# A fixed order with the last token group's output pairs at the end, norm arithmetic on ScalarE, and ten warm-up matmuls instead of fifteen

## The chip, the cores and the metric

The kernel runs on one core of one Trainium2 chip. The metric is device time in microseconds of one execution. Engines are named as in the profile: PE (TensorE, with PEld for its weight loads), DVE (VectorE), ACT (ScalarE), POOL (GpSimd) and SP (SyncE, which only issues DMAs here).

## The reference

Two branches read the same x = `A_q` of 2048 tokens by 640 columns (B_x is not read). One is a long convolution along the tokens, done in the kernel by matrix products with folded Fourier matrices; the other is a token-shifting MLP with two norms. A gate per token mixes them.

```python
kv = (4-tap shift convolution of k with shift_k) * v
y = irfft(rfft(kv padded to 2S) * rfft(ssm_k padded)) [:S] + kv * ssm_D
a = q * y

h = gelu(layernorm(x) @ w1)          # 640 x 640
hs = concat(four column quarters of h, shifted by +1, -1, +2, -2 tokens) @ w2
x1 = x + hs
b = x1 + gelu(layernorm(x1) @ w3) @ w4   # 640 x 1536, 1536 x 640

g = sigmoid((x * gate_w).sum(-1))
return g * a + (1 - g) * b           # x is A_q in both branches
```

## The kernel before

The kernel does not issue instructions directly. Its functions record operations (`P.op`, `P.dma`) with what they read and write; each gets a number in the order of recording. `SEQUENCE`, a list of these numbers written into the source, is the order in which the operations are put on their engines. Each engine works strictly in that order, and waits on semaphores for what its next operation needs. In the kernel before, `schedule` walks the list with estimated durations to choose a PSUM bank for each result, and to hold some large loads behind an earlier transfer; the estimates change nothing else.

Tokens are worked in 16 tiles of 128 (t), in groups of four (sc or c). The columns of the convolution come in two halves of 320 (g or hh). The steps that the change and the prediction touch are these.

- Constants and warm-up: fifteen 512-column matmuls on a buffer of ones (line 715), a first Gelu that loads ScalarE's table (718), and `taps` (four-tap weights spread over partitions by PE).
- `ln1`, `bn_math`: the first norm. DVE's statistics (857, 858), then variance plus epsilon on DVE or POOL (674), then the power -0.5 on POOL (861). `mm1` multiplies by w1. ACT applies Gelu; the fifth block of 128 rows goes to a buffer `hx`, from which DVE copies four 32-row pieces to their shifted places (924).
- `mm2`, `ln2`: w2, x1 and its sums. In `ln_math` POOL makes the mean and a product, DVE the difference, POOL the power; for tiles 8 and up POOL also makes an offset. Then the normed rows go to SP's transposing DMA.
- `mm3`, `mm4`: w3 with Gelu, w4. `base` scales x1 by (1 - g) and stores it, and `mm4`'s result is added to it in memory by an accumulating DMA from POOL's queue. Where a half of a tile is not "summed" there, PE adds x1 with an identity matmul, and the row is kept on the chip.
- `kv_half`, `kv_block`, `x_fwd`, `combine`: the taps and products on DVE, a flip by PE, the forward transform. `h_load`, `h_fold`, `h_chunk`: the same for the filter.
- `unit(hh, c)`: the block products in the frequency domain, all large DVE operations.
- `final(hh, c, q, k)`: the inverse transform of a pair of token tiles by PE, ACT's copy, DVE's sum and difference, a flip by PE, ACT's scaled copy, and DVE's product with q. For k under 12 the pair is added in memory by POOL's accumulating DMA; the last four add X on DVE and are stored by SP.

All DVE tensor-tensor operations have line 669, all matmuls of `mm` line 689, all ACT activations of `act` line 679, all tensor-scalar operations of `ts` line 674, all DMA issues line 237. The transposes of `ln1` on PE have line 903, and the addition of x in `mm2` line 959.

Of the kernel before, what the change touches and what calls it, by code (L numbers as in the profile page):

```python
# [12 lines left out]
class Op:  # L13
    __slots__ = ("idx", "eng", "fns", "ins", "outs", "dur", "bias", "nbytes", "preds", "succs", "rank",
                 "tp", "early", "cost", "free", "grp", "tile", "ordinal", "waits", "inc", "value", "dsem", "dval", "snap", "snapd", "start", "end", "order", "lat")

    def __init__(self, idx, eng, fns, ins, outs, dur, bias, nbytes):
        self.idx = idx
        self.eng = eng
        self.fns = fns  # L20
        self.ins = ins
        self.outs = outs
        self.dur = dur
        self.bias = bias
        self.nbytes = nbytes
        self.preds = {}
        self.succs = []
        self.inc = False
        self.dsem = None
        self.tp = False  # L30
        self.early = False
        self.cost = 0.0
        self.lat = 0.0
        self.free = None
        self.tile = None
# [87 lines left out]
def regions(ap):  # L123
# [30 lines left out]
    for lo, hi in runs:  # L154
        b0, b1 = (f0 + lo) * esz, (f0 + hi) * esz
        for q in range(p0 // 32, (p0 + pcnt - 1) // 32 + 1):
            out.add(("SB", q, b0, b1))
# [16 lines left out]
class Prog:  # L174
# [51 lines left out]
    def dma(self, queue, out, in_, bias=0.0, transpose=False, slow=False, free=None, early=False, accum=False, fn=None):  # L226
# [11 lines left out]
        issue = (350.0 + n / 90.0) if transpose else (970.0 if queue == "pool" else 470.0)  # L238
# [5 lines left out]
        op.cost = n * esz / 256 * 1.65 if transpose else n * esz / run * ((46 + 0.087 * run) if accum else (8 + 0.0435 * run)) / 16  # L244
        op.lat = 1150.0 if transpose else 3000.0 if accum else 2300.0
# [8 lines left out]
    def edges(self):  # L254
        out = []
        for o in self.ops:
            row = []
            for p in o.preds:
                q = self.ops[p]
                if q.nbytes:  # L260
                    d = 60.0
                elif q.eng == o.eng:
                    d = 0.0 if o.eng == "pe" else 120.0
                else:
                    d = {"pe": 205.0, "dve": 120.0, "act": 130.0, "pool": 60.0, "sp": 60.0}[q.eng]
                    d += {"pe": 65.0, "pool": 60.0}.get(o.eng, 0.0)
                row.append((p, d))
            out.append(row)
        return out

    def schedule(self, sequence, backlog=3000.0):
        ops = self.ops
        delays = self.edges()
        free = {"pe": 1580.0, "act": 720.0, "dve": 930.0, "pool": 1190.0, "sp": 720.0}
        dfree = 0.0
        done = []
        avail = [0.0] * 8
        tenant = [None] * 8
        todo = {t.idx: len(t.users) for t in self.banks}
        last = {t.idx: 0.0 for t in self.banks}  # L280
        order = []
        for i in sequence:
            o = ops[i]
            st = max([free[o.eng]] + [ops[p].end + d for p, d in delays[i]])
            if o.nbytes and not o.tp and not o.early:
                st = max(st, dfree - backlog)
            t = o.tile
            if t is not None and t.place is None:
                free_at = {b: max(avail[b:b + t.n]) for b in range(0, 8, t.n)}
                st = max(st, min(free_at.values()))  # L290
                assert st < 1e17, "no bank"
                t.place = min((avail[b ^ 1] <= st if t.n == 1 else False, a, b) for b, a in free_at.items() if a <= st)[2]
                for b in range(t.place, t.place + t.n):
                    if tenant[b] is not None:
                        for u in tenant[b].users:
                            if ops[u].eng != "pe":
                                o.preds.setdefault(u, False)
                    tenant[b] = t
                    avail[b] = 1e18
            o.start = st  # L300
            free[o.eng] = st + o.dur
            o.end = st + o.dur
            if o.nbytes:
                dfree = max(st + 0.5 * o.dur, dfree) + o.cost
                o.end = max(dfree, o.end) + o.lat
                if o.cost > 500 and not o.tp and not o.early:
                    gate = [(ops[d].end, d) for d in done if ops[d].end <= st]
                    if gate:
                        o.preds.setdefault(max(gate, key=lambda g: g[0])[1], False)
                done.append(i)  # L310
            if t is not None:
                todo[t.idx] -= 1
                last[t.idx] = max(last[t.idx], o.end)
                if todo[t.idx] == 0:
                    for b in range(t.place, t.place + t.n):
                        avail[b] = last[t.idx] + 195.0
# [147 lines left out]
def bass_gated_mix__ssm_conv_h3__mixer_s_mlp__prompt_kernel(  # L464
# [33 lines left out]
    def ps(n, cls):  # L498
# [3 lines left out]
    SEQUENCE = [2, 3, 10, 11, 12, 31, 6, 57, 8, 1, 13, 14, 15, 16, 17, 18, 19, 20, 21, 22, 23, 24, 25, 7, 9, 0, 4, 28, 5, 56, 29, 63, 58, 64,  # L502
                59, 27, 141, 30, 60, 35, 61, 52, 65, 62, 76, 66, 26, 80, 67, 34, 77, 42, 68, 78, 70, 146, 53, 82, 69, 71, 43,
                44, 46, 83, 79, 48, 50, 73, 81, 142, 321, 72, 47, 144, 301, 74, 75, 96, 205, 98, 86, 97, 84, 39, 87, 36, 143,
                147, 85, 89, 99, 92, 106, 145, 37, 88, 54, 41, 108, 204, 599, 93, 148, 158, 45, 40, 149, 157, 55, 90, 116,
                161, 120, 249, 160, 250, 102, 109, 113, 162, 136, 91, 137, 150, 154, 138, 139, 151, 159, 103, 302, 117, 38,
                140, 94, 112, 114, 107, 322, 303, 219, 304, 122, 305, 121, 130, 163, 118, 164, 165, 600, 49, 115, 155, 131,
                152, 126, 123, 168, 124, 156, 127, 221, 104, 119, 128, 218, 207, 153, 100, 125, 132, 101, 166, 167, 179, 134,
                169, 171, 222, 110, 51, 223, 133, 308, 210, 170, 135, 111, 209, 177, 129, 95, 601, 323, 199, 220, 224, 200,
                33, 206, 266, 306, 172, 324, 606, 185, 307, 208, 607, 602, 175, 176, 193, 187, 201, 105, 328, 202, 180, 181,  # L510
                211, 212, 405, 603, 267, 178, 188, 213, 194, 182, 203, 425, 173, 264, 186, 268, 196, 191, 192, 183, 604, 406,
                407, 174, 184, 251, 426, 415, 198, 631, 318, 416, 608, 319, 214, 263, 427, 609, 408, 252, 409, 610, 225, 435,
                428, 325, 195, 417, 630, 611, 315, 418, 326, 316, 265, 436, 632, 215, 637, 309, 429, 430, 431, 432, 216, 341,
                317, 437, 320, 633, 197, 455, 310, 438, 456, 228, 419, 638, 605, 226, 327, 311, 634, 612, 217, 445, 420, 189,
                457, 254, 269, 446, 458, 229, 253, 270, 635, 312, 255, 639, 613, 313, 338, 227, 190, 342, 339, 447, 661, 314,
                459, 460, 461, 343, 448, 365, 465, 340, 329, 330, 615, 614, 344, 410, 640, 236, 421, 466, 238, 345, 641, 32,
                616, 642, 237, 331, 256, 346, 663, 367, 617, 664, 257, 662, 366, 239, 636, 234, 668, 242, 235, 232, 258, 665,
                233, 411, 348, 467, 230, 385, 347, 369, 243, 332, 333, 666, 241, 261, 240, 643, 259, 670, 244, 245, 468, 246,
                247, 370, 644, 335, 336, 412, 475, 692, 248, 231, 334, 671, 645, 337, 296, 271, 476, 672, 469, 485, 260, 477,
                478, 507, 669, 508, 368, 387, 509, 273, 693, 479, 262, 699, 371, 449, 357, 486, 627, 628, 629, 487, 358, 359,  # L520
                673, 386, 496, 497, 624, 498, 480, 646, 372, 701, 422, 360, 481, 361, 389, 625, 626, 667, 489, 413, 362, 674,
                675, 353, 354, 356, 450, 451, 694, 618, 619, 355, 390, 423, 349, 620, 350, 363, 364, 373, 272, 274, 374, 700,
                279, 452, 351, 695, 676, 621, 462, 439, 440, 622, 375, 352, 658, 659, 648, 280, 696, 470, 388, 697, 275, 283,
                677, 655, 660, 647, 623, 441, 442, 702, 289, 290, 291, 292, 704, 652, 276, 424, 653, 656, 414, 443, 284, 705,
                649, 650, 703, 678, 706, 651, 287, 657, 732, 392, 293, 285, 433, 277, 698, 654, 391, 278, 471, 707, 294, 281,
                733, 402, 282, 295, 286, 472, 708, 709, 689, 297, 288, 298, 690, 679, 403, 518, 396, 397, 519, 404, 300, 482,
                734, 710, 434, 711, 680, 739, 735, 691, 713, 511, 512, 720, 444, 530, 721, 740, 736, 681, 398, 453, 737, 712,
# [457 lines left out]
    def summed(hh, t):  # L985
        return 8 * hh + 2 * (3 - t // 4) < KACC
# [200 lines left out]
```

## Time and profile before

| | |
|---|---|
| median of 3 runs | 235.57 us (234.06 to 236.06) |
| the profiled execution | 235.56 us, its span 233.8 us |
| PE busy | 221.1 us, 95% of the span |
| DVE busy | 220.1 us, 94% |
| ACT busy | 170.3 us, 73% |
| POOL busy | 105.9 us, 45% |
| granted TensorE clock, mean | 0.994 |
| DMA moved | 45.48 MB, 195 GB/s in the mean |

The span runs from the first instruction to the end of the last; the 1.8 us beside it are not in the trace. Busy time counts overlapping instructions of an engine once. PE's busy time is modelled from the starts of its matmuls. POOL's row includes its DMA issues, 40 of 1.2 us each.

### The profile page before, as it was taken

How to read it: one execution, taken by the hardware profiler on the slowest of the kernel's cores; microseconds unless marked ns; L12 is line 12 of the kernel's file. 1: busy time of each engine (PE TensorE's matmuls, PEld its weight loads, DVE VectorE, ACT ScalarE, POOL GpSimd, SP SyncE). 2: the span in 40 equal slices, each digit the busy share in tenths (PEclk: the TensorE clock that was granted, in tenths of full speed). 3: DMA queues.
4: the chain of work that ended last, by engine and by line, in shares of the span. 5: the costliest groups of instructions: out<-in, count | busy, mean ns of one | idle time of the engine just before them, and what ended most of it. 6: DMA issues, size and time to landing. Idle time of an engine off the chain costs nothing.

```text
span 233.8 us, 4171 instructions
## 1 busy us (share of the span) xinstructions
PE 221.1 (95%) x1501; PEld 134.6 (58%) x1501; DVE 220.1 (94%) x402; ACT 170.3 (73%) x317; POOL 105.9 (45%) x122
## 2 busy tenths in 40 slices
PE   7999999989998999999999999999999999999960
PEld 2598665436554656544775456654666556776630
DVE  6998999999988999998999999999989999979994
ACT  2799699488796899769949897577655387288881
POOL 0330406274495801196376693246024332456870
PEclk9999999999999999999999999999999999999997
DMA  5999959898878999978638988999978987989998
GB/s 161 360 345 250 253 146 271 246 277 204 140 181 176 240 213 317 343 212 180 157 97 145 187 189 163 146 191 206 259 142 145 196 140 142 185 98 111 95 109 165
DMA packets 63785, 45.48 MB, mean 195 GB/s; under 512 B 28818, under 2 KB 59028, under 8 KB 63764
## 3 DMA queue, kind: packets, MB, share of 16 engines
q1 hardware_dynamic: 54748, 33.33, 55.2%
q0 software_dynamic: 8832, 11.80, 34.9%
q8 instruction: 12, 0.20, 0.3%
q10 hardware_dynamic: 184, 0.08, 0.1%
q14 instruction: 9, 0.07, 0.1%
HBM read 24.22 MB, written 6.55 MB: 132 GB/s over the span
## 4 chain that ended last, share of the span: by engine, by line
PE 45%; DVE 9%; POOL 3%; ACT 2%; issue 1%
PE PSall L689 45%; DVE arena L669 8%; ACT arena L679 2%; POOL arena L674 1%; POOL arena L861 1%; POOL arena L669 1%; DVE arena L959 0%; DVE arena L674 0%
## 5 line engine op out<-in xcount | busy, mean ns | idle before, releaser
L689 PE MATMUL PSall<-arena 128*128 128x320 bf16 (+5 forms) x1444 | 213.7, 307 | 5.3 <-DVE arena L669 2.4
L669 DVE TENSOR_TENSOR arena<-arena 128x640 bf16<-128x640 bf16 (+5 forms) x247 | 182.3, 793 | 3.0 <-ACT arena L679 1.9
L689 PEld LDWEIGHTS PSall<-arena 128*128 128x128 bf16 (+1 forms) x1444 | 130.5, 98 | 86.9 <-DVE arena L669 4.2
L679 ACT ACTIVATE arena<-PSall 128x512 bf16<-128x512 f32 (+6 forms) x189 | 107.7, 634 | 29.4 <-PE PSall L689 25.2
L679 ACT ACTIVATE arena<-arena 128x640 bf16<-128x640 bf16 (+4 forms) x62 | 42.2, 703 | 6.7 <-POOL arena L669 2.7
L861 POOL TENSOR_TENSOR arena<-arena 128x1 f32<-128x1 f32 (+1 forms) x26 | 29.3, 1128 | 31.9 <-DVE arena L674 31.5
L674 POOL TENSOR_SCALAR arena<-arena 128x1 f32<-128x1 f32 (+2 forms) x41 | 24.8, 608 | 34.7 <-DVE arena L959 12.0
L237 POOL DMA_DIRECT2D out_dram<-arena x28 | 30.5, 1197 | 20.5 <-ACT arena L679 15.0
L679 ACT ACTIVATE arena<-PSall,arena 128x640 bf16<-128x640 f32 (+1 forms) x32 | 20.6, 658 | 20.0 <-PE PSall L689 19.9
L237 POOL DMA_DIRECT2D arena<-arena x12 | 14.9, 1242 | 32.1 <-DVE arena L669 28.2
L674 DVE TENSOR_SCALAR arena<-arena 128x640 bf16<-128x640 bf16 (+2 forms) x49 | 14.4, 307 | 3.4 <-POOL arena L674 1.6
L857 DVE BATCH_NORM_STATS2 arena<-arena 128x6 f32<-128x320 bf16 x32 | 14.6, 479 | 2.0 <-DMA arena<-in_A_q_dram 1.7
L669 POOL TENSOR_TENSOR arena<-arena 128x1 f32<-128x1 f32 (+1 forms) x11 | 10.3, 943 | 2.9 <-DVE arena L674 2.5
L715 PE MATMUL PSall<-arena 128*128 128x512 bf16 x15 | 5.4, 536 | 1.6 <-DVE arena L711 1.6
L959 DVE SCALAR_TENSOR_TENSOR arena<-PSall,arena 128x640 bf16<-128x640 f32 x8 | 6.4, 808 | 0.1
L924 DVE TENSOR_SCALAR arena<-arena 32x256 bf16<-32x256 bf16 (+1 forms) x24 | 5.9, 244 | 0.5
L679 ACT ACTIVATE PSall<-PSall 128x640 f32<-128x640 f32 x8 | 5.6, 699 | 0.1
L715 PEld LDWEIGHTS PSall<-arena 128*128 128x128 bf16 x15 | 1.9, 132 | 4.6 <-issue 2.5
L903 PE MATMUL PSall<-arena 128*128 128x128 bf16 x40 | 3.6, 219 | 0.3
L718 ACT ACT_TABLE_LOAD x1 | 1.3, 1283 | 2.7 <-issue 2.7
L903 PEld LDWEIGHTS PSall<-arena 128*128 128x128 bf16 x40 | 2.4, 97 | 1.4 <-DVE arena L858 0.4
L858 DVE BATCH_NORM_AGGREGATE arena<-arena 128x2 f32<-128x12 f32 x16 | 3.0, 197 | 0.0
(24 smaller groups left out, 9.6 us busy)
## 6 DMA issues: line engine op xcount, KB each, us to landing
arena<-arena POOLq DMA_DIRECT2D x12, 640.0 KB, 6.3
arena<-in_A_k_dram SPq DMA_DIRECT2D x14, 400.0 KB, 4.1
arena<-in_A_q_dram SPq DMA_DIRECT2D x14, 320.0 KB, 6.9
out_dram<-arena POOLq DMA_DIRECT2D x20, 160.0 KB, 4.2
arena<-in_A_ssm_k_dram SPq DMA_DIRECT2D x5, 512.0 KB, 4.4
arena<-in_A_v_dram SPq DMA_DIRECT2D x16, 160.0 KB, 3.9
arena<-in_B_w_dram SPq DMA_DIRECT2D x1, 1920.0 KB, 8.8
out_dram<-arena SPq DMA_DIRECT2D x10, 160.0 KB, 3.7
```

Source lines behind the costliest of these rows:

```text
L237: fn = lambda e: e.dma_start(out, in_, **kw)
L669: P.op(eng, lambda e: e.tensor_tensor(o, real(a), real(b), op), [a, b], [o], dve_ns(o, [a, b], 2) if eng == "dve" else 500)
L674: P.op(eng, lambda e: e.tensor_scalar(o, real(a), s1, s2, op0=op0, **({} if op1 is None else {"op1": op1})), [a] + aps, [o], dve_ns(o, [a] ...
L679: P.op("act", lambda e: e.activation(real(o), real(a), f, bias=bias, scale=scale, **({"accum_out": accum} if accum is not None else {})), ...
L689: fns.append(lambda e, l=l, r=r, i=i: e.matmul(real(o), l, r, start=(i == 0), stop=(i == last)))
L715: P.op("pe", lambda e: e.matmul(real(pw), warm[:, 0:128], warm[:, 128:640], start=True, stop=True), [warm], [pw], 427.0 if i < 14 else 216.0)
L857: P.op("dve", lambda e, o=o, i=i: e.bn_stats(o, i), [i], [o], 400)
L858: P.op("dve", lambda e: e.bn_aggr(bna[:, t, :], bns[k]), [bns[k]], [bna[:, t, :]], 120)
L861: P.op("pool", lambda g: g.tensor_tensor(o, a, e, ALU.pow), [a, e], [o], dur)
L903: P.op("pe", [lambda e, c=c, pb=pb, xn=xn: e.transpose(real(pb)[:, 128 * c:128 * (c + 1)], xn[:, 128 * c:128 * (c + 1)], ident) for c in r ...
L924: P.op("dve", lambda e, o=hT[q, 4, c0:c0 + n], i=hx[q, :]: e.tensor_scalar(o, i, 1.0, None, op0=ALU.mult), [hx[q, :]], [hT[q, 4, c0:c0 + n ...
L959: P.op("dve", lambda e: e.scalar_tensor_tensor(x, real(pr), 1.0, x, op0=ALU.mult, op1=ALU.add, accum_out=st[1, 0][:, t:t + 1]), [pr, x], [ ...
```

## The change

The change has these parts.

1. Ten warm-up matmuls instead of fifteen (`WARM`).
2. The arithmetic between sums and power goes to ACT: in `rsqrt` ACT adds epsilon, and POOL keeps only the power; in `ln_math` ACT makes the mean, the combination of sums and the addition; for tiles 8 and up ACT makes the offset. The factors 1/sqrt(640) move from ACT's squares into the Gelu of `mm3`, as constants.
3. In the last two token groups (sc 2 and 3) Gelu's fifth block is written by four ACT operations straight from PSUM to the shifted places, without `hx` and the DVE copies.
4. The output. Every tile under 12 is stored by `base` as a full row and added to by `mm4` in full rows; the last token group (tiles 12 to 15) is not stored by `base`, gets x1 by identity matmuls for both halves, and its four pairs (k 12 to 15: group 3 of both halves) come last, add X on DVE and are stored by SP. Before, the last four pairs were groups 1 and 0 of the second half.
5. A new `SEQUENCE`, and a new list `PLACES` that names each result's PSUM bank. The walk with durations goes, and with it the holding of loads behind earlier transfers. The durations that are still recorded with each operation are changed, but nothing reads them when the kernel is built.
6. Each Gelu is recorded as reading what the table load wrote, and pieces of SBUF are tracked in steps of four bytes.

```diff
@@ -152,7 +155,7 @@
-        b0, b1 = (f0 + lo) * esz, (f0 + hi) * esz
+        b0, b1 = (f0 + lo) * esz // 4 * 4, ((f0 + hi) * esz + 3) // 4 * 4
@@ -251,69 +261,21 @@
-    def schedule(self, sequence, backlog=3000.0):
...
-                if o.cost > 500 and not o.tp and not o.early:
-                    gate = [(ops[d].end, d) for d in done if ops[d].end <= st]
-                    if gate:
-                        o.preds.setdefault(max(gate, key=lambda g: g[0])[1], False)
...
+    def schedule(self, sequence, places):
         tenant = [None] * 8
...
+        for t, b in zip(self.banks, places):
+            t.place = b
         order = []
         for i in sequence:
-            o = ops[i]
...
+            o = self.ops[i]
             t = o.tile
...
+            if t is not None and tenant[t.place] is not t:
                 for b in range(t.place, t.place + t.n):
                     if tenant[b] is not None:
                         for u in tenant[b].users:
...
+                            if self.ops[u].eng != "pe":
                                 o.preds.setdefault(u, False)
                     tenant[b] = t
@@ -706,14 +678,14 @@
-    WARM = 15
+    WARM = 10
@@ -857,20 +829,19 @@
-    def pool_pow(o, a, e, dur=900):
-        P.op("pool", lambda g: g.tensor_tensor(o, a, e, ALU.pow), [a, e], [o], dur)
+    def rsqrt(o, a, b, i, dur=1200):
+        act(a, b, ACTF.Identity, bias=epsc[:, i:i + 1])
+        P.op("pool", lambda e: e.tensor_tensor(o, a, neghalf[:, 0:n_of(o)], ALU.pow), [a, neghalf], [o], dur)
 
     def bn_math(t0, t1):
         for a, b in ((t0, t1),) if t0 >= 4 else ((t, t + 1) for t in range(t0, t1)):
-            ts(st[0, 3][:, a:b], bna[:, a:b, 1], 1e-5, None, ALU.add, eng="dve" if a < 4 else "pool")
-            pool_pow(st[0, 5][:, a:b], st[0, 3][:, a:b], neghalf[:, a:b], 750)
+            rsqrt(st[0, 5][:, a:b], st[0, 3][:, a:b], bna[:, a:b, 1], 0, 650 if t0 < 4 else 1200)
 
     def ln_math(l, t):
         s = {f: st[l, f][:, t:t + 1] for f in range(6)}
-        ts(s[2], s[0], -1.0 / D, None, ALU.mult, eng="pool")
-        ts(s[4], s[2], s[2], 1e-5, ALU.mult, ALU.subtract, eng="pool")
-        ts(s[3], s[1], s[4], None, ALU.subtract)
-        pool_pow(s[5], s[3], neghalf[:, t:t + 1])
+        act(s[2], s[0], ACTF.Copy, scale=-1.0 / D)
+        act(s[4], s[0], ACTF.Identity, scale=s[2], bias=s[1])
+        rsqrt(s[5], s[3], s[4], 1)
@@ -917,12 +888,17 @@
             else:
+                if sc >= 2:
+                    for g in range(4):
+                        c0, q = 2 + SHIFT[g] + t0, slice(32 * g, 32 * (g + 1))
+                        act(hT[q, 4, c0:c0 + n], pr[q, :], ACTF.Gelu_apprx_tanh)
+                    continue
                 hx = hxb[t0 // 256 % 2][:, 0:n]
@@ -954,11 +930,11 @@
-            act(pr, pr, ACTF.Square, scale=D ** -0.5, accum=st[1, 1][:, t:t + 1])
+            act(pr, pr, ACTF.Square, accum=st[1, 1][:, t:t + 1])
@@ -969,7 +945,7 @@
-        tt(off, mean, rstd, ALU.mult, eng="pool")
+        act(off, mean, ACTF.Copy, scale=rstd)
@@ -978,18 +954,19 @@
-            act(uT[:, ft, :], pr, ACTF.Gelu_apprx_tanh)
+            act(uT[:, ft, :], pr, ACTF.Gelu_apprx_tanh, scale=D ** 0.5)
 
     KACC = 12
 
     def summed(hh, t):
-        return 8 * hh + 2 * (3 - t // 4) < KACC
+        return t < 12
 
     def tile_rows(t):
-        n = 640 if summed(1, t) else 320
-        return X[:, t, 0:n], out[0, 128 * t:128 * (t + 1), 0:n]
+        return X[:, t, :], out[0, 128 * t:128 * (t + 1), :]
 
     def base(t):
+        if t >= 12:
+            return
@@ -1001,8 +978,9 @@
-        x, o = tile_rows(t)
-        P.dma("pool", o, x, accum=True)
+        if t < 12:
+            x, o = tile_rows(t)
+            P.dma("pool", o, x, accum=True)
@@ -1148,12 +1126,15 @@
-    for hh in range(2):
-        for c in (3, 2, 1, 0):
-            for q in range(2):
-                at(final, hh, c, q, 8 * hh + 2 * (3 - c) + q)
-
-    sched = P.schedule(SEQUENCE)
+    k = 0
+    for group in ((2, 1, 0), (3,)):
+        for hh in range(2):
+            for c in group:
+                for q in range(2):
+                    at(final, hh, c, q, k)
+                    k += 1
+
+    sched = P.schedule(SEQUENCE, PLACES)
```

Read through the numbering, the new list orders the operations so. SP loads the tokens of tiles 0 to 5 first, then the two halves of w1 (the lower columns first), as before with other neighbours. The four transposes of tiles 0 to 3 and the tap matmuls stand around the first `mm1`; the bulk of w2 is the seventeenth issue on SP, where it was the thirteenth. The sums and differences of the six pairs of the first half's groups 2 to 0 stand among the products of `unit(1, 3)` on DVE; before, all pairs stood behind them. The last large matmul group on PE is `mm4` of tile 14, with two flips behind it. The last four DVE operations are the second tiles of the pairs k 14 and k 15, and the last six issues on SP are stores, as before.

## The prediction

> **What bounds the kernel now.** I read the page's engine row first, then the table by stretches of ten microseconds, then the chain that ended last, then the waits of PE and DVE, and last the groups by form for prices.
>
> ```profile
> PE 221.1 (95%) x1501; PEld 134.6 (58%) x1501; DVE 220.1 (94%) x402; ACT 170.3 (73%) x317; POOL 105.9 (45%) x122
> ```
>
> Two engines are nearly full and a third is not far off. In the table the columns are PE, PEld, DVE, ACT and POOL busy, then the granted clock, the DMA share and GB/s.
>
> ```profile
> 0.00:10.00 10.00, 8.23 (x47) 3.72 (x47) 7.13 (x33) 4.11 (x8) 2.36 (x8) 1.00 0.81 235
> 10.00:20.00 10.00, 9.87 (x161) 8.81 (x159) 9.31 (x31) 9.69 (x30) 2.27 (x5) 1.00 1.12 352
> ...
> 40.00:50.00 10.00, 9.12 (x48) 4.42 (x47) 9.51 (x21) 6.12 (x10) 4.55 (x6) 1.00 0.92 230
> ...
> 70.00:80.00 10.00, 9.06 (x73) 5.34 (x72) 9.38 (x21) 7.21 (x12) 7.03 (x10) 1.00 0.87 183
> ...
> 160.00:170.00 10.00, 10.00 (x59) 5.60 (x58) 10.00 (x12) 6.08 (x12) 1.62 (x3) 1.00 0.96 225
> ...
> 210.00:220.00 10.00, 9.71 (x72) 6.64 (x71) 9.90 (x22) 8.69 (x17) 7.07 (x7) 1.00 0.96 104
> 220.00:230.00 10.00, 6.15 (x42) 3.50 (x39) 9.70 (x30) 7.66 (x16) 6.68 (x6) 1.00 1.05 119
> ```
>
> PE's 12.7 us without work are four things: 1.6 before the first warm-up matmul, 3.1 scattered between 10 and 110 us (0.88 and 0.94 of it in the stretches shown), 2.5 between 210 and its last matmul at 228.3, and 5.4 after that. Between 110 and 210 it never stops. DVE stands at 10.00 there too.
>
> ```profile
> 106.61 102.03 PE PSall L689 x640
> 208.64 0.02 issue
> 208.66 0.54 ACT arena L679
> ...
> 212.61 4.04 DVE arena L669 x10
> ...
> 222.03 2.09 PE PSall L689 x14
> ...
> 230.45 0.32 DVE arena L669
> ```
>
> The chain (start, length, engine, line) is one unbroken run of PE for 102 us and then, from 209, mostly DVE. So PE sets the time up to about 208 and DVE the last 22 us. A cheaper DVE pays only in that end; before it, only PE's own work or its waits count.
>
> **The change, part by part.** The sum is made against the profiled execution, 235.56 us (span 233.8 and 1.8 around it); the median of the three runs is 235.57, so it needs no correction.
>
> *Warm-up and start.* Five 512-column matmuls go.
>
> ```profile
> 1.64 5.36 PE L715 MATMUL PSall<-arena 128*128 128x512 bf16 x15 [1.64 <-DVE arena L711]
> ...
> 5.46 1.04 PEld L715 LDWEIGHTS PSall<-arena 128*128 128x128 bf16 x5 [0.28 <-issue]
> ...
> 10.00 0.33 DVE L737 TENSOR_SCALAR arena<-arena 128x640 bf16<-128x640 bf16 x1 [0.43 <-DMA arena<-in_B_w_dram]
> ```
>
> After 5.46 they stand 0.21 apart, so five are 1.1 us. But they are not what holds the first `mm1`, which stands at 9.13: its weights are the sixth and seventh load on SP's queue in both orders, and the second half lands only at 10.0 (line 737 waits for it). Ahead of 9.13 PE does transposes and tap matmuls, and the new order puts the same ones there. The first weight half is issued 0.5 before the second, so it can be used from about 8.5 to 9.1. Gain 0 to 0.6; I take 0.4. Cover gone, the removed matmuls would be worth 1.1.
>
> The first nine warm-ups stand 0.43 apart and the rest 0.21: PE's rate doubled after 3.8 us. The Trainium skill, "TensorE: Matmul & The Clock Gate", Part 1, says the half-rate phase is about 3.4 us of time in a free-running window, not a number of matmuls. By that rule ten warm-ups barely cover it, and an unlucky window would run four tap matmuls at half rate too, 4 x 0.21 = 0.9 us; the start term would then be 0 and not -0.4. The trace of before shows one phase only.
>
> *Norm arithmetic to ScalarE.* The prices are in the groups by form (busy, mean ns, then idle before):
>
> ```profile
> L861 POOL TENSOR_TENSOR arena<-arena 128x1 f32<-128x1 f32 x20 | 24.6, 1232 | 31.5 <-DVE arena L674 31.5
> L674 POOL TENSOR_SCALAR arena<-arena 128x1 f32<-128x1 f32 x32 | 19.4, 609 | 16.5 <-DVE arena L959 12.0 <-ACT arena L679 2.8
> L674 DVE TENSOR_SCALAR arena<-arena 128x1 f32<-128x1 f32 x20 | 3.9, 194 | 2.8 <-POOL arena L674 1.6 <-ACT arena L679 1.2
> L924 DVE TENSOR_SCALAR arena<-arena 32x512 bf16<-32x512 bf16 x8 | 2.3, 287 | 0.2
> L679 ACT ACTIVATE arena<-arena 128x16 f32<-128x16 f32 x1 | 0.2, 207 | 0.0
> ```
>
> POOL loses 32 + 8 small products and six additions, some 30 us by its rows, and keeps the 26 powers; at 45% it bounds nothing, so that is worth nothing by itself. DVE loses 20 small operations (3.9) and the waits in front of them (2.8). ACT gains 48 (three for each of 16 tiles) + 8 (offsets) + 10 (first norm) = 66 one-column activations. The nearest ACT row costs 0.207; a scale or bias from memory adds 0.09 (the 640-column copy from PSUM is 790 ns with one, 702 without). That gives 16 x 0.207 + 16 x 0.38 + 34 x 0.295 = 19.5 us end to end. Activations overlap: all of ACT's, by count times mean, make 25 us more than its 170.3 busy, 0.08 each. So at least 14.2. As each tile's three depend on one another, I take 17.
>
> A rule that would make the gain larger: the Trainium skill, "SBUF — State Buffer", section "SBUF: two separate sides", says VectorE and GpSimd share a port pair under an exclusive lock and the loser blocks fully. By it DVE, too, would be freed of blocks by POOL's small products; PE's work allows no more than the first rival's 228.6 for that. Here the loser is POOL: its powers take 0.7 to 4.2 us, while DVE's 2560-column operations take 1.48 to 1.52 with POOL at work or not. So DVE's term holds only its own rows.
>
> *Shifted Gelu writes.* For the last two 512-token groups two activations of 0.60 become eight, and eight DVE copies go (2.3). ACT +6 x 0.60 = 3.6 (3.1 overlapped): a one-row activation of 320 columns costs 0.45, about what 128 rows do, so fewer rows save nothing.
>
> *Base and final.* Sixteen scaled copies and stores of X become twelve full rows: ACT 16 copies (8 x 0.82 + 8 x 0.56 = 11.0) to 12 x 0.82 = 9.9, SP four stores fewer, POOL four accumulating issues of 1.2 fewer, the bytes alike. PE's eight identity matmuls stay eight, now all on the last token group. DVE adds X for four pairs as before. The six last stores on SP stay six.
>
> *DVE's end.* In sum DVE does 6.2 us less (4.0 if each removed operation was overlapped by 0.08) and loses up to 2.8 of waits. Up to 208 PE covers that; past it DVE sets the pace, and PE's 2.5 us of waits in that end are what a DVE 4 to 9 us earlier can give back. I take all 2.5. Bounds: 0 if PE's new order is itself late, 2.5. After the last matmul DVE now needs 2.4 us. In the new order the last big matmul group (`mm4` of tile 14) comes just ahead of the last two flips, so ACT does its 0.79, then 0.53 + 0.53, then DVE four short operations: about 2.1. Gain 0.3 (0 to 0.8). The 3.0 of the last store stay.
>
> *PE's waits between 10 and 110.* Of these 3.1, 0.9 is one wait on a DVE line-674 operation at 72.5, a gate read that stood in a row of shift copies; with the copies gone I count it as gone. Against it stands the fuller ACT: from 10 to 130 its busy times add to 97.8 of 120, and 17 + 3.4 - 1.1 = 19 us come in, nearly all there, which leaves 3 us of slack. PE needs ACT to empty its banks. I put 0.5 for that, from 0 to 11 (below).
>
> **Sum:** -0.4 - 0.9 + 0.5 - 2.5 - 0.3 = -3.6; 235.6 - 3.6 = **232.0 us**.
>
> **The rivals.**
>
> *All of PE's waits go* (chance 0.17): -0.6 - 3.1 - 2.5 - 0.8 = -7.0, so 228.6. For it: the written order is new everywhere, and DVE has reserve in front of every inverse transform. Against it: PE had 3.1 us of waits with a less loaded ACT.
>
> *The start is DMA's, and the gain is spent there* (0.20): the DMA share is 1.12 from 10 to 20 us. The new order reaches the first `mm2` after 16 x 0.28 + 5 x 0.55 + 4 x 0.28 and small ones, 9.1 us of PE work behind the first `mm1`, so near 18 us instead of 22. The bulk of w2 (640 KB) was the thirteenth issue on SP; now it is the seventeenth, with 280 KB more ahead of it, 1 us at the stretch's 352 GB/s. Loads of weights landed up to 8.7 us after issue there, so it comes at about 17.5. Half a microsecond of slack. If it and the constants behind it (Rh, behind two transposes on SP) are late by 1.5 each, 3 us are lost and the time is 235.0, within 1%.
>
> *ScalarE becomes the bound* (0.21), the other side: between 10 and 130 us ACT goes from 97.8 to 114 (all overlapped) or 120 (none) of 120. In before it waited 45 us for PE in the whole run, so half of its 22 us of idle time in this stretch is likely forced by order. If 11 of idle must stay, it ends the stretch 5 to 11 us late, PE stands behind full banks, and from there PE has no slack to 210. It decides from where forced idle exceeds the 3 us left. Taking 6 on top of the forecast: 238.0. Against it: the small ones mostly stand between larger activations, where overlap holds, and their operands are early.
>
> **How the numbers follow.** Forecast 0.42 (230.3 to 233.2), waits gone 0.17, DMA start 0.20, ScalarE 0.21. One per cent, 2.4 us, is about what a measurement tells here (the three runs of before lie 2.0 apart). Faster 0.42 + 0.17 = 0.59, same 0.20, slower 0.21. The range goes from just under the best case, 228.0, to just over the slow one, 238.5; the first-weight bound, 0.6, and the upper half of ACT's price lie in the two tenths outside.
>
> **What would show it.** Right: PE at 9.9 or more in every stretch from 110 to 215, PE's idle time after 210 under 1 us ahead of its last matmul, no POOL line-674 group but the gate's, DVE busy near 214, ACT near 190. First `mm1` near 8.7. Wrong: PE waits for ACT of several us between 20 and 130 (ScalarE rival), or for a load between 15 and 35 (DMA rival); PE's last matmul later than 227; DVE still 3 us behind it at the end.

## The result and the profile after

The changed kernel took 246.48 us (median of 4 runs, 245.63 to 247.31) and the kernel before 235.41 on the same chip: a ratio of 1.048, 95% interval 1.042 to 1.054. In a later timing, perhaps on another chip (the first one's is not known), the same two kernels took 240.02 (238.89 to 240.57) and 235.62, 1.017 (1.013 to 1.021). So the change made the kernel slower, by 1.7 to 4.8%, and the size is part of what has to be explained. The experiments ran on four chips, and the changed kernel itself was timed only these two times. The kernel before was timed beside them on each chip and gave 235.4 to 235.8 everywhere, so ratios to it can be compared.

The profiled execution is one of 246.41 us with a span of 244.5. In the page's engine row DVE and POOL have lost what the change took from them, ACT has gained 14.8 us, and PE's "busy" has grown by 5 us without more matmuls.

```profile
PE 226.4 (93%) x1496; PEld 137.9 (56%) x1496; DVE 216.0 (88%) x376; ACT 185.1 (76%) x385; POOL 72.0 (29%) x72
```

In the table by stretches (PE, PEld, DVE, ACT, POOL busy, granted clock, DMA share, GB/s) the waits that the kernel before had at 40-50 and 70-80 us are gone, and so are those after 210. Everything lost lies in two places: the first 20 us, where the granted clock falls, and 120 to 160 us.

```profile
0.00:10.00 10.00, 6.96 (x32) 2.92 (x32) 6.78 (x31) 4.68 (x10) 2.72 (x8) 0.88 0.78 239
10.00:20.00 10.00, 10.00 (x142) 9.72 (x142) 7.97 (x31) 8.38 (x30) 1.48 (x2) 0.78 1.08 341
40.00:50.00 10.00, 10.00 (x72) 5.47 (x71) 10.00 (x22) 9.93 (x24) 5.60 (x7) 1.00 1.17 230
70.00:80.00 10.00, 10.00 (x64) 6.00 (x63) 9.86 (x19) 9.40 (x18) 0.00 (x0) 1.00 1.08 225
120.00:130.00 10.00, 7.47 (x47) 4.30 (x44) 9.96 (x9) 4.80 (x10) 7.97 (x3) 1.00 0.54 84
130.00:140.00 10.00, 8.22 (x26) 3.23 (x27) 9.93 (x8) 7.75 (x18) 2.88 (x5) 0.66 0.52 98
140.00:150.00 10.00, 7.95 (x50) 4.64 (x48) 4.71 (x5) 3.97 (x9) 1.54 (x2) 1.00 1.24 70
150.00:160.00 10.00, 6.62 (x30) 3.25 (x31) 3.78 (x3) 7.67 (x15) 2.69 (x3) 0.66 0.79 179
160.00:170.00 10.00, 10.00 (x67) 6.33 (x65) 10.00 (x11) 3.69 (x6) 2.37 (x2) 1.00 1.03 202
210.00:220.00 10.00, 10.00 (x67) 6.33 (x66) 9.96 (x9) 2.92 (x5) 5.91 (x7) 1.00 1.04 167
```

Between 120 and 160 PE stands still for 9.7 us (40 less the four busy times) and runs 8.22 and 6.62 us at a mean granted clock of 0.66, which loses another 0.34 x 14.84 = 5.0. Together 14.7 us, about the whole distance between the forecast and the result. Neither ACT nor PE is full there: ACT is busy 24.2 of the 40 us.

The chain that ended last (start, length, what) names what stood in the way: a power on POOL (line 834) of 7.14 us, and two transposing DMAs (`arena<-arena`) of 5.71 and 10.12. After them PE runs unbroken to its last matmul.

```profile
122.06 0.08 issue
122.14 7.14 POOL arena L834
129.28 0.02 issue
129.31 0.30 ACT arena L649
...
130.58 5.71 DMA arena<-arena
136.29 0.02 issue
136.31 0.84 ACT arena L649 x2
...
140.21 10.12 DMA arena<-arena
150.33 0.02 issue
150.36 0.84 ACT arena L649 x2
...
153.38 85.65 PE PSall L659 x542
239.04 0.02 issue
239.06 0.80 ACT arena L649
```

All three end in ACT (line 649). The timeline of ACT (start, length, operation; in brackets the idle time before it and what ended it) shows its three stops. They are the offset of tile 12 in `ln2`, which waits for tile 12's power, and the squares of tiles 14 and 15.

```profile
129.31 1.25 ACT L649 ACTIVATE arena<-arena 128x1 f32<-128x1 f32 x2 [5.13 <-POOL arena L834]
...
136.31 0.74 ACT L649 ACTIVATE arena<-arena 128x640 bf16<-128x640 bf16 x1 [2.19 <-DMA arena<-arena]
...
150.36 0.74 ACT L649 ACTIVATE arena<-arena 128x640 bf16<-128x640 bf16 x1 [6.39 <-DMA arena<-arena]
```

The squares wait for a DMA because of what they throw away. `act(xn2[t % 2], X[:, t, :], ACTF.Square, ...)` wants only the sum; its 640 columns of output go to `xn2[t % 2]`, the buffer from which the transposing DMA of tile t-2 still reads. Behind the waiting instruction, in ACT's fixed order, stand copies and Gelus that would empty PSUM banks, and PE runs out of banks. PE's two stops both end with such an ACT operation, a Gelu of `mm3` and a copy:

```profile
131.78 16.17 PE L659 MATMUL PSall<-arena 128*128 128x512 bf16 x74 [4.31 <-ACT arena L649]
...
153.38 6.89 PE L659 MATMUL PSall<-arena 128*128 128x320 bf16 x30 [5.43 <-ACT arena L649]
```

That it is the bank and not the data is read from the program: the matmuls that start there read nothing that these operations write. The kernel before had these instructions too, but in its order ACT waited for transposes 0.5 us once and for POOL 2.7 us in two waits.

### The profile page after: what moved, and what is told of

It reads as the page before. It is cut to its first block, busy times and chain, and to the rows that moved or that the text cites. A ratio compares the mean times of both kernels' runs of the same rounds, so it can differ in the third digit from the quotient of the medians.

```text
span 244.5 us, 4098 instructions
## 1 busy us (share of the span) xinstructions
PE 226.4 (93%) x1496; PEld 137.9 (56%) x1496; DVE 216.0 (88%) x376; ACT 185.1 (76%) x385; POOL 72.0 (29%) x72
## 4 chain that ended last, share of the span: by engine, by line
PE 68%; ACT 14%; DMA 11%; POOL 3%; DVE 2%; issue 1%; SPq 0%
PE PSall L659 67%; ACT arena L649 14%; DMA arena<-arena 9%; POOL arena L834 3%; DMA arena<-in_A_q_dram 2%; PE PSall L874 1%; DVE arena L829 1%; DVE arena L638 1%; SPq L240 0%; DVE arena L643 0%; DVE arena L830 0%; PE PSall L724 0%
## 5 line engine op out<-in xcount | busy, mean ns | idle before, releaser
L659 PE MATMUL PSall<-arena 128*128 128x320 bf16 (+5 forms) x1444 | 220.8, 314 | 10.5 <-ACT arena L649 9.9
L659 PEld LDWEIGHTS PSall<-arena 128*128 128x128 bf16 (+1 forms) x1444 | 133.7, 100 | 95.6 <-ACT arena L649 14.3
L649 ACT ACTIVATE arena<-PSall 128x512 bf16<-128x512 f32 (+7 forms) x195 | 112.4, 629 | 14.8 <-PE PSall L659 13.5
L649 ACT ACTIVATE arena<-arena 128x1 f32<-128x1 f32 (+4 forms) x124 | 60.1, 505 | 19.7 <-DMA arena<-arena 8.9
L834 POOL TENSOR_TENSOR arena<-arena 128x1 f32<-128x1 f32 (+1 forms) x26 | 27.9, 1077 | 104.0 <-ACT arena L649 103.9
L240 POOL DMA_DIRECT2D out_dram<-arena x24 | 27.2, 1360 | 27.2 <-DVE arena L638 14.5
L643 DVE TENSOR_SCALAR arena<-arena 128x640 bf16<-128x640 bf16 (+1 forms) x29 | 11.1, 385 | 0.1
L900 DVE TENSOR_SCALAR arena<-arena 32x256 bf16<-32x256 bf16 x16 | 3.5, 216 | 2.2 <-ACT arena L649 1.9
L687 PE MATMUL PSall<-arena 128*128 128x512 bf16 x10 | 3.6, 535 | 1.6 <-DVE arena L683 1.6
L643 POOL TENSOR_SCALAR arena<-arena 128x16 f32<-128x16 f32 x3 | 3.0, 1008 | 4.9 <-ACT arena L649 4.9
```

The lines of the kernel that those rows point to most:

```text
L240: fn = lambda e: e.dma_start(out, in_, **kw)
L643: P.op(eng, lambda e: e.tensor_scalar(o, real(a), s1, s2, op0=op0, **({} if op1 is None else {"op1": op1})), [a] + aps, [o], dve_ns(o, [a] ...
L649: P.op("act", lambda e: e.activation(real(o), real(a), f, bias=bias, scale=scale, **({"accum_out": accum} if accum is not None else {})), ...
L659: fns.append(lambda e, l=l, r=r, i=i: e.matmul(real(o), l, r, start=(i == 0), stop=(i == last)))
L687: P.op("pe", lambda e: e.matmul(real(pw), warm[:, 0:128], warm[:, 128:640], start=True, stop=True), [warm], [pw], 427.0 if i < 9 else 216.0)
L834: P.op("pool", lambda e: e.tensor_tensor(o, a, neghalf[:, 0:n_of(o)], ALU.pow), [a, neghalf], [o], dur)
```

## The experiments

All are edits of the changed kernel, except one of the kernel before. "PE lost" is the time between the starts of consecutive matmul groups less their length at full rate, added up over a stretch; it counts both standing still and half rate.

**The unwanted output goes elsewhere.**

```diff
-    oR = alloc(2048)
+    oR = alloc(2176)
-        act(xn2[t % 2], X[:, t, :], ACTF.Square, accum=st[1, 1][:, t:t + 1])
+        act(V(oR + 1536, 640), X[:, t, :], ACTF.Square, accum=st[1, 1][:, t:t + 1])
```

> The squares of the second norm (tokens from tile 8 on) write their unwanted output to a buffer of their own instead of xn2[t % 2]. Theory (ScalarE stands in its order behind the write after read on that buffer, while transposing DMAs land late): ScalarE's waits for DMA arena<-arena go from 8.9 to under 1 us, PE's wait of 5.6 us at 148 and the half-rate groups after it (2.2 us) go, time 238.5-240.5. Rival (ScalarE has too much work in 120-160): its waits go, but the work behind them is only done in the same time, PE still waits for ScalarE; time 245-246.5. Second rival (the late landing itself is what costs): the wait comes back at the next use of the late tile, time 243-245.

Measured: 237.96 us (10 runs, 236.28 to 241.85), 2 to 8.5 us less than the changed kernel in its two timings; it was not timed beside this run. ACT no longer waits for any transpose, and from 140 us to its last matmul PE is hardly idle:

```profile
120.00:130.00 10.00, 6.82 (x42) 3.81 (x39) 9.93 (x9) 4.83 (x10) 8.30 (x2) 1.00 0.55 82
130.00:140.00 10.00, 8.87 (x28) 3.48 (x29) 9.96 (x8) 8.67 (x20) 4.76 (x4) 0.66 0.67 123
140.00:150.00 10.00, 10.00 (x65) 6.21 (x64) 4.79 (x5) 8.60 (x18) 2.02 (x3) 1.00 0.81 174
```

The second stall was the buffer. ACT does the same work (184.9 us against 185.1), so it was not load. The first stall, 4.5 us and then 2.9 at half rate, is untouched.

**Tile 12's offset, apply and transpose later in the order.** In `SEQUENCE` their numbers (558, 559, 560) move behind that of tile 13's `ln_math` (567), so that ACT comes to them after the copies, Gelus and squares it used to leave waiting.

```diff
-... 809, 558, 892, 559, 877, ... 566, 560, 934, 854, 567, 890, ...
+... 809, 892, 877, ... 566, 934, 854, 567, 558, 559, 560, 890, ...
```

> Only the order is changed: the product and the apply of the second norm of tile 12, and its transposing DMA, stand 8 places later in ScalarE's order, behind the evictions of mm4 t2 and xf11.0, the Gelus of mm3 and the squares of tile 13. Theory (the 5.1 us in which ScalarE waits for GpSimd's power of tile 12 stops evictions that stand behind it): that wait is under 1 us, PE's gap of 4.3 us at 127.5 and the 2.8 us of half-rate groups after it go, time 239-241.5. Rival (load): PE waits for ScalarE just as long, time 245.5-246.5. Second rival: the power comes still later and the wait only moves: 243-246.

Measured: 240.52 us (238.90 to 246.21), inside what the changed kernel itself gives in its two timings. The wait for the power fell to 0.6 us, but the later transpose landed later, the squares of tile 14 waited 5.8 us for it, and PE lost about 8 us from 130 us on. So the wait moved, though not as the second rival had it: the power did not come later, the transpose did. Alone, this run decides nothing on the time.

**Both.**

> Both of the two edits before together (own buffer for the squares' unwanted output, and the later place of tile 12's product and apply). Theory: the two stalls are separate and their sum is had: 246.5 less 12 to 15, 231.5-234.5, with the granted clock at 1.0 from 20 us on. If one stall hides behind the other, 237-240. Rival (ScalarE's load): 243-246.

Measured: 232.48 us (231.74 to 233.23), 0.984 of the kernel before (0.979 to 0.990). PE lost 3.1 us in all after the first 20 us. With both stops out of ACT's way the rest of the change is worth 3 us.

**Fifteen warm-ups.** The five extra matmuls ride in the last warm-up operation.

```diff
-        P.op("pe", lambda e: e.matmul(real(pw), ...), [warm], [pw], ...)
+        P.op("pe", [lambda e: e.matmul(real(pw), ...)] * (1 if i < 9 else 6), [warm], [pw], ...)
```

> Fifteen warm-up matmuls again (the five extra ones ride in the last warm-up operation), everything else as changed. If the loss of the first 20 us (PE time lost against full rate: 4.4 us in 0-10 and 2.0 us in 10-20, against 2.8 and 0.6 before) comes from the shorter warm-up, the groups of five 128-column matmuls around 9 to 13 us take 0.28 us again instead of 0.53, and the time falls by 2 to 3 us, to 243.5-244.5. If it comes from the gaps in which PE waits for the constants' loads and for w1, they stay at 0.53 and the time moves by less than 0.5 us. The stalls at 126, 146 stay in both.

Measured: 241.95 us (239.88 to 242.93). The 128-column matmuls of `mm1` between 9 and 16 us take 219 ns here and 290 in the changed kernel:

```profile
L659 PE MATMUL PSall<-arena 128*128 128x128 bf16 x58 | 4.4, 219 | 0.2 <-ACT arena L649 0.2
...
L659 PE MATMUL PSall<-arena 128*128 128x128 bf16 x46 | 5.4, 290 | 0.0
...
L599 PE MATMUL PSall<-arena 128*128 128x128 bf16 x45 | 4.6, 268 | 0.2 <-ACT arena L589 0.2
```

The third line is from another kernel with fifteen warm-ups, the last of this section: its profiled execution has a granted clock of 0.50 from 11.03 to 14.44 us. All eleven traces with ten warm-ups lose 0.9 to 2.0 us of PE between 10 and 20 us; of the five with fifteen only that one has half rate there, and it loses 1.7. So the shorter warm-up brings half rate at the start each time here, but fifteen do not rule it out. And this run's last ACT wait was 3.4 us and not 6.4, so its time can't be laid to the warm-up.

**The changed kernel again, unaltered.**

> The changed kernel again, unaltered, on the chip of the runs beside it. If what differs between chips and executions is small, 245.5-247.5 us, the same two losses of PE (about 7 us from 126, about 8 us from 146) and 128-column matmuls at half rate from 9 to 13 us. If the last of the three losses depends on when DMAs happen to land, it is between 3 and 8 us here and the time from 242 on.

Measured: 240.02 us. The wait for POOL is the same 5.1 us; the three waits for transposes together are 5.1 us, the longest 2.2, where the first trace has 8.9 and 6.4. By the landing records tile 13's transpose took 4.9 us from issue here, 7.0 in the run with fifteen warm-ups and 10.1 in the first trace. That accounts for most of the difference between the two traces: PE lost 1.8 us from 140 to 160 instead of 7.8. After the 1.0-us gap at 146 us in this trace the granted clock stayed at 1.00; after the first trace's gaps of 4.3 and 5.4 us it read 0.50 for 6.83 us each. The Trainium skill, "TensorE: Matmul & The Clock Gate", section "Why this matters for your kernels", says to leave no idle gaps of over about 3 us between bursts of matmuls. These two gaps agree, but shorter ones cost the clock here too: it read 0.50 for 3.41 us behind a gap of 2.74 us (to 150.39, the run with fifteen warm-ups) and behind one of 1.99 us (to 24.26, the run below with the norms alone on ACT). Between 20 and 210 us every gap of PE from 1.99 us up in the sixteen traces was followed by half rate, and none of 1.5 us or less was. So a gap under 3 us is not safe by these traces.

**Why the transposes land late.** GpSimd issues two accumulating DMAs (`mm4`'s of tile 2 and `unit` 02's first, 640 KB) just ahead of tile 13's transpose. Here they come behind the power of tile 15:

```diff
-... 819, 878, 848, ... 904, 907, 811, ... 986, 590, 899, ...
+... 819, 848, ... 904, 811, ... 986, 590, 878, 907, 899, ...
```

> The changed kernel with two accumulating DMAs (mm4's of tile 2 and unit02's first) issued by GpSimd behind the power of tile 15, so that none is in flight when tile 13's transposing DMA is issued. Theory (a transposing DMA lands late because it shares the queues with accumulating ones): it lands 2.6 us after its issue instead of 4.9 to 10.1, ScalarE's wait before the squares of tile 15 is under 0.5 us instead of 2.2 to 6.4, PE's loss at 146 (1.0 to 5.6 us) goes; tile 12's, issued behind unit03's second accumulating DMA, still takes 5.7. Time 238-240 on a chip where the changed kernel gives 240, 238-240 as well where it gives 246.5. Rival (transposes are slow at that time whatever else is in flight): 4.9 us or more, time unchanged. What it costs: unit02's first sum comes some 10 us later, which VectorE feels if it has nothing else to do (2 to 4 us).

Measured: 239.49 us (238.17 to 241.88). Tile 13's transpose landed after 2.58 us, the wait ahead of tile 15's squares is gone, and PE lost 0.3 us from 140 to 160. Tile 12's, issued 1.4 us behind an accumulating DMA as before, took 5.61 again, and ACT still waited 2.1 for it. So the accumulating DMAs are what made tile 13's late. They are not the whole story: by the landing records some transposes land in 2.6 to 2.7 us beside an accumulating DMA (tiles 12 and 13 of the kernel before in 2.57 and 2.60), and some take 5.8 to 10.1 with only loads in flight (at 94 and 100 us in the changed kernel). Why tile 13's took 4.9 us in one trace of the changed kernel and 10.1 in the other stays open; the four runs of each timing lie within 2 us of one another, which speaks against chance from one execution to the next. The time itself can't be told apart from the 240.0 us that the changed kernel took in its second timing.

**What holds the power.** In the timeline of DVE and POOL (a row of instructions without a pause is one line), POOL's power of tile 12 stands 7.13 us, although the shortest of that line in the same trace takes 0.55.

```profile
118.68 11.70 DVE L638 TENSOR_TENSOR arena<-arena 128x640 bf16<-128x640 bf16 x12
...
122.14 7.13 POOL L834 TENSOR_TENSOR arena<-arena 128x1 f32<-128x1 f32 x1 [2.03 <-ACT arena L649]
```

DVE is in one unbroken row of two-input operations there, and its first place without overlap, where a sum waits for the product ahead of it, is at 128.85; the power ends 0.4 us later. Lengths on POOL are rough in a profile, but ACT's operation that waits for the power starts 0.03 us behind its end, at 129.31. Three runs add one VectorE operation of two elements to the kernel with the buffer of its own (237.96 us). In two of them it reads the product just made, so that it also waits. The first edit (1284 is the new operation):

```diff
-... 558, 892, 559, ...
+... 558, 892, 1284, 559, ...
...
+    u = P.ops[892].outs[0]                    # unit03's U0; 893 is U1
+    u = bass.AP(AR, u.offset, [list(u.ap)[0], [1, 2]])
+    P.op("dve", lambda e: e.tensor_scalar(bfs[:, 44:46], u, 1.0, None, op0=ALU.mult), [], [], 70).preds[892] = True
```

> Own buffer for the squares' unwanted output, as in the run that gave 238.0 us, and one added VectorE operation of two elements, behind unit03's U0 and waiting for it, so that VectorE has a short gap at about 124 us in its row of overlapping operations. Theory (GpSimd's power of tile 12 is held from its start until VectorE's first gap): the power ends at about 124 instead of 128.6, takes 2 us instead of 7.1, ScalarE's wait of 5.1 us and PE's losses at 125-138 (7.3 us) go, time 230.5-233. Rival (the power is long for a reason of its own, or its wait is not what PE feels): it stays 7 us long, 237-239.

Measured: 230.61 us (230.13 to 231.07), 0.978 of before (0.976 to 0.981). In the timelines of this and the next two kernels the order is written in one line, so line 774 is the power and 578 DVE's two-input operations:

```profile
118.54 4.82 DVE L578 TENSOR_TENSOR arena<-arena 128x640 bf16<-128x640 bf16 x6
...
121.60 2.19 POOL L774 TENSOR_TENSOR arena<-arena 128x1 f32<-128x1 f32 x1 [2.03 <-ACT arena L589]
...
123.40 0.17 DVE L1079 TENSOR_SCALAR arena<-arena 128x2 bf16<-128x2 bf16 x1
```

The power ends at 123.79, just behind the added operation.

> The same added operation one product later, behind U1. Theory: the power ends with VectorE's gap at about 127.1, so it takes 5.3 to 5.7 us, ScalarE's wait is 3.3 to 3.8 us, PE's gap is shorter by 1.4 us: 235-236.5. Rival: 7.1 us and 237-239.

Measured: 234.71 us in one run. The power began at 120.78, the added operation at 126.11, the power ended at 126.50: 5.72 us long. PE lost 4.4 us from 120 to 140.

> The same small operation at the first place, but reading constants and waiting for nothing, so that VectorE's row has one more operation and no gap. Theory: the power still takes about 7.1 us and ends near 128.7, time as without it, 237-239. Rival (any small operation of this kind lets GpSimd in): the power ends near 124 and the time is 230.5-233.

Measured: 230.06 us in one run. The rival is right here. The added operation overlaps the product ahead of it, so DVE has no gap, and the power is let in all the same:

```profile
120.74 2.20 POOL L774 TENSOR_TENSOR arena<-arena 128x1 f32<-128x1 f32 x1 [2.04 <-ACT arena L589]
...
122.42 0.17 DVE L1077 TENSOR_SCALAR arena<-arena 128x2 bf16<-128x2 bf16 x1
122.50 8.07 DVE L578 TENSOR_TENSOR arena<-arena 128x1280 bf16<-128x1280 bf16 x6
```

So it is not a gap that the power needs, but an end to the row of two-input operations: a one-input operation of 0.17 us in the row does. The Trainium skill, "SBUF — State Buffer", section "Who interferes with whom", says that a VectorE instruction with two SBUF inputs contends with a GpSimd one that reads SBUF, and that one with at most one SBUF input (outside some modes) does not; the three ends of the power, 123.79, 126.50 and 122.94, each 0.2 to 0.4 us behind the added operation, agree, though no run shows in which mode that operation ran. It speaks of a lock for one instruction, though, and here it outlasted a row of them: the power waited through five product and sum operations of 0.8 to 1.5 us.

**Where the arithmetic runs.** First the norms' small operations go back to POOL and DVE in the new order, then they alone go to ACT in the old one.

> The new order, banks and shifted Gelus as changed, but the norms' 66 small operations back on GpSimd and VectorE. Theory (the order is what stands wrong: ScalarE's apply of tile 12 and the squares of tiles 14 and 15 stand ahead of evictions and wait): ScalarE still waits for GpSimd at 124 and for transposes, GpSimd's chain has three more steps for each tile beside VectorE's long operations, so 245-252. Rival (the arithmetic on ScalarE, 17 us more of its time, is what makes PE wait): ScalarE busy 168 us, PE's losses at 120-158 under 4 us together, time 230-236.

Measured: 248.23 us (248.15 to 248.68), 1.054 of before (1.051 to 1.057); ACT busy 173.4 us. Less work on ACT did not help. By itself that does not refute load, as other waits came in with this edit; what does is that ACT does the same work, 185.0 us, in the run with both edits (232.48 us). The time came within the theory's range, but by another road: from 100 to 160 us ACT waited only 3.6 us for POOL, and DVE 15.9 us for ACT's squares, since the difference of the sums stands in DVE's order again.

> The kernel before with its own order, banks and fifteen warm-ups; only the norms' small operations are on ScalarE. Theory (ScalarE has room, 167 us of 233; what costs is only what stands behind a wait): ScalarE busy about 184, waits for GpSimd's powers of 1 to 4 us a tile at the later tiles, of which PE feels little: 234-239. Rival (ScalarE's load or its latency is what cost 11 us): 241-248, with PE waiting for ScalarE between 20 and 160.

Measured: 239.96 us (239.56 to 241.50), 1.020 of before (1.017 to 1.023), just outside the theory's range. ACT busy is 183.7, so the arithmetic costs ACT 13.4 us. Of PE's extra loss of 4.4 us, 3.6 lie between 20 and 30 us, and the timeline of ACT shows the same pattern, an epsilon waiting for DVE's statistics ahead of Gelus:

```profile
23.64 0.30 ACT L865 ACTIVATE arena<-arena 128x2 f32<-128x2 f32 x1 [2.12 <-DVE arena L860]
...
26.10 0.30 ACT L865 ACTIVATE arena<-arena 128x2 f32<-128x2 f32 x1 [1.18 <-DVE arena L860]
```

From 60 to 210 us it loses under 1 us more than the kernel before. In this trace the longer ACT row costs where the order puts a wait ahead of evictions, and little elsewhere.

**Versions that beat both kernels.** The buffer, tile 12 later and fifteen warm-ups:

> The two edits of the run before (232.5 us) and fifteen warm-up matmuls. If the start's loss of clock, 1.8 us between 10 and 20 us, is on the path to the end, 230.5-231.5. If PE only waits longer for the next load or for ScalarE (as in the run with fifteen warm-ups alone, where 1.4 us came back as a wait at 103 us), 232-233.

Measured: 230.43 us (229.97 to 232.48), 0.980 of before (0.976 to 0.984). Then the buffer and the small VectorE operation, with ten and with fifteen warm-ups on one chip:

> Ten warm-up matmuls, own buffer for the squares' unwanted output, and the small VectorE operation that waits for nothing behind unit03's U0: the kernel that gave 230.1 us in one run, timed. 229.5-231 us; PE loses 0.6 to 1.9 us to half-rate matmuls between 10 and 20 us.

> The same with fifteen warm-up matmuls. If the shorter warm-up costs what PE loses at half rate, 0.8 to 1.9 us less than with ten: 228-229.5. If the start is bound by the loads, the same within 0.5 us: 229.5-231. The prediction's own term (ten start PE 0.4 us earlier) would have it 0.4 us slower.

Measured: 230.18 us (229.66 to 230.88), 0.977 of before (0.974 to 0.980), with ten; 229.68 (228.61 to 232.43), 0.975 (0.971 to 0.979), with fifteen. The difference of 0.5 us is not resolved; the profiled execution with fifteen (232.43 us) is the one with half rate at the start. In the kernel with ten, the stretch that cost 14.7 us is full (the same columns as above):

```profile
120.00:130.00 10.00, 10.00 (x59) 5.46 (x57) 9.93 (x10) 9.70 (x21) 4.69 (x3) 1.00 0.82 154
130.00:140.00 10.00, 10.00 (x60) 5.77 (x59) 9.96 (x8) 9.83 (x22) 4.53 (x5) 1.00 0.69 148
```

The end of its chain is one run of PE and ACT's last copies:

```profile
114.13 109.27 PE PSall L599 x700
223.40 0.02 issue
223.42 0.80 ACT arena L589
```

## Why the prediction was wrong

The forecast was 232.0, the range 228.0 to 238.5; measured were 246.48 and, in the later timing, 240.02. With ACT's stops taken out, the rest of the change gives 230.2 with ten warm-ups. So the other terms held in sum, some of them by errors of opposite sign, and a stretch that had no term decided.

- *The step that failed* is "between 110 and 210 it never stops". That is a reading of the old order, and it was carried over to the new one. The sum looked for waits behind a fuller ACT from 10 to 130 us (+0.5, 0 to 11) and had nothing for 120 to 160, where 14.7 us went. The third rival (ScalarE the bound, 238.0) had the right engine and the wrong mechanism: it costed load, and ACT was busy 24 of those 40 us. What counted was what each waiting instruction on ACT has behind it.
- *"POOL ... bounds nothing, so that is worth nothing by itself", "here the loser is POOL".* The port rule was weighed for DVE alone. (The powers there take 0.56 to 4.18 us and DVE's 2560-column operations 1.42 to 1.52, a little wider than the 0.7 to 4.2 and 1.48 to 1.52 that it read; that changes nothing in it.) The 4.2-us power in the trace of before was the warning; the question left out was who waits for that power once the offset is ACT's. The answer was 5.1 us of ACT, 4.5 of PE and 2.8 of half rate.
- *The squares' output.* No step asked whether the new order leaves the transposes time to land. Before, they landed in about 2.6 us there and ACT hardly waited; in the new order the squares of tile 15 stood 3.8 us behind tile 13's transpose in ACT's time, and that transpose took 4.9 to 10.1 us.
- *Norm arithmetic on ACT*: taken at 17 us (14.2 to 19.5); it measures 13.4 in the old order (183.7 less 170.3) and 11.7 in the new one (185.1 less 173.4), since the small activations overlap more than 0.08 each. The rows of before bear that out: by count times mean they add up to 28 us above the busy time, 0.09 each and not 0.08, which would have put the lower bound at 13.6. ACT's busy time was put near 190; it is 185.
- *Start*, -0.4: wrong sign. PE's first `mm1` stands at 9.27, before at 9.13, forecast about 8.7. Ahead of it PE waited 1.1 us in two waits for DVE (line 643, the normed rows that it transposes) and ran at half rate, so it was not the first half of w1 that held it. The matmuls behind it run at half rate until about 14 us, which loses 2.0 us between 10 and 20 us in the first trace and about 1.5 in its repetition; the traces with fifteen warm-ups in this order lose 0.3, 0.2 and 1.7. The rule quoted from the Trainium skill, "TensorE: Matmul & The Clock Gate", Part 1, pointed there; by the prediction's working it cost up to 0.9. Against it stand 1.1 us of removed matmuls; the net of 0.5 between ten and fifteen was not resolved.
- *PE's waits from 10 to 110*, -0.9 + 0.5: too small. Of the 3.1 us of waits some 0.2 are left, as the first rival had it: from 20 to 120 us PE is busy 99.75 of 100 us. The fuller ACT cost nothing there.
- *DVE's end*, -2.5 and -0.3: right within 0.3. PE's waits ahead of its last matmul are 0.3 us, before 2.5 after 210; after that matmul 2.0 us are left, before 2.4. DVE's busy time was put near 214; it is 216.0, lower by 4.1, which is what its removed rows give when overlapped (4.0).
- *DMA start* (second rival): did not come; PE has no wait for w2 in any stretch after 20 us.

## What to carry to other kernels

When small work moves to an engine that works in a fixed order, price the waits and not the work: list for each moved instruction what it waits for and what stands behind it that another engine needs. An output that nobody reads still takes a buffer, and a write after read on it can stop an engine; give it a place of its own. A reading such as "PE never stops here" belongs to one order and says nothing of the next.

## What the runs showed of the hardware

A 128x1 power on GpSimd was held for 7.13 us by a row of overlapping two-input VectorE operations, through several of them, and one 0.17-us one-input operation in that row freed it, worth 7 us of the whole kernel (237.96 to 230.61 and 230.06). Transposing DMAs of 128x640 landed 2.6 to 10.1 us after their issue; moving two accumulating DMAs away brought one of them from 4.9 to 10.1 down to 2.58, but other traffic delays them too. Half rate lasted 3.41 or 6.83 us each time between 20 and 210 us, and followed gaps of PE from 1.99 us up. The granted clock in the windows does not always show half rate: the kernel with ten warm-ups has 1.00 from 0 to 20 us, but its 128-column matmuls between 8 and 14 us take 304 ns on average, much as in the changed kernel (312), whose clock reads 0.50 there. That trace's first record of the clock is at 13.67 us, and ahead of it the windows read 1.00 all the same.
